# Preparing the first unit of a fused convolution and gated MLP: convolution by bands and then turning, against turning and then diagonal taps on TensorE

## Chip, cores and metric

One core of a Trainium2 chip. The metric is the device time of one execution in microseconds; three runs of the kernel before took 705.06 to 705.57, median 705.33.

## The reference

x is (8, 4096, 192), weight (8 heads, 7 taps), w_in (192, 2048), w_out (2048, 192), all float32. In short:

```python
w = softmax(weight, axis=-1)                       # 8 heads x 7 taps
# causal convolution in time; channel d belongs to head d // 24
c[b, s, d] = sum_k w[d // 24, k] * x_padded[b, s + k, d]   # 6 zeros ahead of each sequence
h = c.reshape(32768, 192) @ w_in                   # 32768 x 2048
out = (h * cos(h)) @ w_out                         # 32768 x 192
```

## The kernel before

The 32768 tokens are cut into 32 units of 1024 (U) and each unit into two tiles of 512 tokens (T), so there are 64 tiles. x arrives token-major (128 tokens on the partitions). For the product with w_in the convolved unit must stand channel-major, in the tile cT (64 channels on each half of the partitions, three groups k of 64 channels). Units 0 to 3 are prepared in one way and later units in another; the change concerns unit 0 and the constants that are made before it.

A tile then runs as follows. mm1 (L503) makes eight products h0 to h7 of w_in with cT, six matmuls each on alternate halves of the rows, into an h buffer; there are three such PSUM buffers ("the ring"), which parts of convolutions use in turn too. ACT takes the sine of h + pi/2 (L510, "s0" to "s7"), DVE multiplies it with h into g (L514). mm2 (L552) multiplies g with w_out (wo, bfloat16, in two halves, cast from wo_f by POOL at L120, steps W0 and W1) in 64 steps a tile ("m12" is twelve steps); two PSUM banks of 512 columns (o_bank 0 and 1) hold its sums. Steps 0 to 15 of a tile need the first half of wo, step 16 the second.

The order on each engine is written out by hand. PE_FIRST and PE_ORDER list what PE is given, ACT_FIRST and ACT_ORDER what ACT and DVE are given, tile by tile; engines run their queues in order. Tokens used below: hN is mm1 number N (h0a, h0b its halves), m the mm2 steps, w filler products, K the casts of a unit of x by POOL (L219), W the casts of wo, d and c the band convolution of a later unit, D, X and Y the doubling, the turning by a DMA transpose and the mending of its edges, L the loads of a unit, r (before) the rest of unit 0's convolution, e with a name the copies out of PSUM that belong to it. The first line of PE_FIRST before is:

```
"K1 h0a h0b W0 h1 h2 h3 r h4 w5 d11 w4 h5 d21 W1 c11 X0 m1 h6 m11 h7 L2 c21 D1"
```

Before the first tile the kernel before does this. The softmax of the taps is made with two heads on each quarter of the partitions (L140 to L185: quarter, wmax, wexp, wsum, wn). prod and diag (L401, L404) form the taps along a diagonal, and sixteen small copies (L415), shared by DVE, POOL and ACT, put them into band, a banded matrix for each head. conv_first (L432) convolves the first four blocks of 128 tokens by 32 products with bands; two copies (L438) bring them to ct, turned by twelve products with an identity (L453) and copied to cT (L457). The other four blocks go through r (conv_rest, L465 and L472) and a DMA transpose X0 (L326). keep_warm (L136) issues products of zeros. w_in is loaded by POOL in two transfers (L112), one for each half of its columns, which are the two halves of the partitions of w. On SP the second half of unit 0 and the whole of unit 1 are released by diag, and w_out (L124) by conv_first's second copy.

Of the kernel before, what the change touches and what calls it, by code (L numbers as in the profile page):

```python
# [16 lines left out]
def kernel(  # L17
# [40 lines left out]

    xf = x.rearrange("b s d -> (b s) d")
# [20 lines left out]
    w_row = consts.tile([4, HQ * K], FP32)  # L80
    nc.scalar.dma_start(out=w_row, in_=weight.rearrange("(q h) k -> q (h k)", q=4))
# [26 lines left out]
    w_src = moe_w_in.rearrange("(m k) (t f) -> t m k f", k=NC, t=2)  # L108
    HP = NP // 2

    def load_w(t):
        nc.gpsimd.dma_start(out=w[64 * t : 64 * t + 64].rearrange("p k j f -> p k (j f)"), in_=w_src[t])  # L112

    load_unit(0, 0, NB)
# [12 lines left out]

    one = consts.tile([128, 1], FP32)
    nc.vector.memset(one, 1.0)
    zero = consts.tile([128, T], BF16)  # L130
    nc.vector.memset(zero, 0.0)  # L131
    idle = o_pools[0].tile([128, T], FP32, name="o_ps0")

    def keep_warm(n, bank=idle):
        for _ in range(n):
# [3 lines left out]
    quarter = consts.tile([4, 128], FP32)  # L139
    nc.gpsimd.memset(quarter, 1.0)  # L140
    nc.gpsimd.affine_select(out=quarter, in_=quarter, compare_op=ALU.is_ge, fill=0.0, base=0, pattern=[[1, 128]],
                            channel_multiplier=-32)
    nc.gpsimd.affine_select(out=quarter, in_=quarter, compare_op=ALU.is_ge, fill=0.0, base=31, pattern=[[-1, 128]],
                            channel_multiplier=32)
# [4 lines left out]
    w_bc = w_all[:, 0 : HQ * K].rearrange("p (h k) -> p h k", k=K)  # L149
    nc.tensor.matmul(out=w_all[:, 0 : HQ * K], lhsT=quarter, rhs=w_row, start=True, stop=True)  # L150
    keep_warm(9)


    xb0 = consts.tile([128, UB + 1, D], BF16, name="x_bf0")

    E = 32 + K - 1
    mask = consts.tile([128, E, K], BF16)
    nc.gpsimd.memset(mask[0:32], 0.0)
    nc.gpsimd.affine_select(out=mask[0:32], in_=mask[0:32], compare_op=ALU.not_equal, fill=1.0, base=1 - K,  # L159
                            pattern=[[1, E], [1, K]], channel_multiplier=-1)  # L160
    band = consts.tile([128, H, 256], BF16)
    nc.vector.memset(band, 0.0)
    for q, copy in enumerate((nc.vector.tensor_copy, nc.scalar.copy, nc.scalar.copy)):
        copy(out=mask[32 * q + 32 : 32 * q + 64], in_=mask[0:32])  # L164
    for t in range(2):
        load_w(t)
    nc.gpsimd.memset(xb0[:, 0, :], 0.0)
    ident = consts.tile([128, 128], BF16)
    nc.gpsimd.memset(ident, 0.0)
    nc.gpsimd.affine_select(out=ident, in_=ident, compare_op=ALU.not_equal, fill=1.0, base=0, pattern=[[1, 128]],  # L170
                            channel_multiplier=-1)
    wn = consts.tile([128, HQ, K], BF16)
    ct_bufs = [consts.tile([128, 2 * NC * NPB + 1, 64], BF16, name="ct_buf%d" % i) for i in range(2)]

    wmax = consts.tile([128, HQ, 1], FP32)
    nc.vector.tensor_reduce(out=wmax[:, :, 0], in_=w_bc, axis=mybir.AxisListType.X, op=ALU.max)
    wexp = consts.tile([128, HQ, K], FP32)
    nc.vector.tensor_tensor(out=wexp, in0=w_bc, in1=wmax.to_broadcast([128, HQ, K]), op=ALU.subtract)
    nc.scalar.activation(out=wexp, in_=wexp, func=AF.Exp)
    nc.scalar.activation(out=scrap, in_=one, func=AF.Sin)  # L180
    wsum = consts.tile([128, HQ, 1], FP32)
    nc.vector.tensor_reduce(out=wsum[:, :, 0], in_=wexp, axis=mybir.AxisListType.X, op=ALU.add)
    winv = consts.tile([128, HQ, 1], FP32)
    nc.vector.reciprocal(winv, wsum)
    nc.vector.tensor_tensor(out=wn, in0=wexp, in1=winv.to_broadcast([128, HQ, K]), op=ALU.mult)  # L185
    wo = consts.tile([128, NP, 2, D], BF16)

# [19 lines left out]
    def cast_unit(u, n0=0, n1=UB + 1, copy=nc.gpsimd.tensor_copy):  # L207
        if u >= FIRST_RAW:
            xk[u] = xk_pool.tile([128, NC * (UB + 1), 64], BF16, name="xk")
            for n0, n1 in ((NPB, UB + 1), (0, NPB)):  # L210
                copy(out=xk[u][:, NC * n0 : NC * n1].rearrange("p (k n) m -> p k n m", k=NC),  # L211
                     in_=x_tiles[u][:, n0:n1].rearrange("p n (m k) -> p k n m", k=NC))
            if u % UPS == 0:
                nc.gpsimd.memset(xk[u][0 : 128 - OP, 0 : NC * NPB : NPB], 0.0)
            return
        if n0 == 0:
            bf[u] = xb0 if u == 0 else xbf_pool.tile([128, UB + 1, D], BF16, name="x_bf")
        o = 1 if u == 0 else 0
        copy(out=bf[u][:, n0 + o : n1 + o, :].rearrange("p n (h k r) -> p (n h) k r", k=NC, r=R),  # L219
             in_=x_tiles[u][:, n0:n1, :].rearrange("p n (h r k) -> p (n h) k r", k=NC, r=R))  # L220

    ct_tiles = {}
    have = {("whole", 0, 0)}
# [24 lines left out]
    def conv_part(u, c, banks, whole=False):  # L248
# [6 lines left out]
        if u == 1 and c == 0:  # L255
            spread_taps(ps[1][:, nb * 2 * G : nb * 2 * G + K])
# [4 lines left out]
        for b in range(2):  # L261
            conv_out(u, c, ps, 0, 0, nb, nc.scalar.copy, banks=(b,))
            if b and u == 1 and c == 0:
                nc.scalar.copy(tap, ps[1][:, nb * 2 * G : nb * 2 * G + K])
# [44 lines left out]
    def turn_unit(u, n0=0, n1=UB + 1, part=0):  # L309
# [12 lines left out]
        have.update((("turn", u), ("whole", u, 1)) if u == 0 else (("turn", u),))  # L322
# [9 lines left out]
    pick = consts.tile([128, 2, 2, 4, 2, R], BF16)  # L332

    def spread_taps(ps):

        for i in range(2):
            nc.tensor.matmul(out=ps, lhsT=pick[:, i].rearrange("p t q i r -> p (t q i r)"), rhs=wn[:, i, :],
                             start=i == 0, stop=i == 1, skip_group_check=True)

# [12 lines left out]
    def taps(u, j, half, mul):  # L352
        if u not in pa:
            pa[u] = pa_pool.tile([128, PA, WN, OR], FP32, name="pa")
        part = slice(HALF * half, HALF * (half + 1))
# [4 lines left out]
    def conv_raw(u):  # L360

        a, p = pa.pop(u), raw_prod
# [26 lines left out]
    def mend_edges(u):  # L389
# [6 lines left out]


    cast_unit(0, 0, NB, nc.scalar.copy)

    prod = consts.tile([128, HQ, E, K], BF16)  # L400
    nc.vector.tensor_tensor(out=prod, in0=mask.rearrange("p (o e) k -> p o e k", o=1).to_broadcast([128, HQ, E, K]),  # L401
                            in1=wn.rearrange("p h (o k) -> p h o k", o=1).to_broadcast([128, HQ, E, K]), op=ALU.mult)
    diag = consts.tile([128, HQ, E], FP32)
    summed = nc.vector.tensor_reduce(out=diag, in_=prod, axis=mybir.AxisListType.X, op=ALU.add)  # L404

    tc.add_manual_dep(nc.sync.nop().ins, summed.ins.name, sync_dep, reason="order of the transfers")
    load_unit(0, NB, UB)
# [3 lines left out]

    three = {"D": nc.vector.tensor_copy, "A": nc.scalar.copy, "P": nc.gpsimd.tensor_copy}
    for i, k in enumerate("DPDPDPDPDPDPDPAA"):
        q, rows = divmod(i, 4)
        three[k](out=band[32 * rows : 32 * rows + 32, HQ * q : HQ * (q + 1), 32 * rows : 32 * rows + E],  # L415
                     in_=diag[32 * q : 32 * q + 32])
    cast_unit(0, NB, UB)
    nc.gpsimd.memset(pick, 0.0)
    for i in range(2):
        nc.gpsimd.affine_select(out=pick[:, i, :, :, i, :], in_=pick[:, i, :, :, i, :], compare_op=ALU.not_equal, fill=1.0,  # L420
                                base=0, pattern=[[0, 2], [-32, 4], [0, R]], channel_multiplier=1)
    ct_tiles[0] = ct_pool.tile([128, UB + 1, NC, 2, 64], BF16, name="ct")
    cT[0] = cT_pool.tile([128, NC * (UB + 1) * 128], BF16, name="cT")
    copies = [nc.scalar.copy, nc.vector.tensor_copy]

    def conv_first():

        banks = o_banks()
        for half in range(2):
            for h in range(H):  # L430
                for prev in range(2):
                    nc.tensor.matmul(  # L432
                        out=banks[half][:, 0 : 2 * D].rearrange("p (n k h r) -> p h n k r", n=2, k=NC, h=H)[:, h],
                        lhsT=band[:, h, 128 * prev : 128 * prev + 128],
                        rhs=bf[0][:, 2 * half + 1 - prev : 2 * half + 3 - prev, h * G : (h + 1) * G].rearrange(
                            "p n (k r) -> p n k r", k=NC),
                        start=(h == 0 and prev == 0), stop=(h == H - 1 and prev == 1), skip_group_check=True)
            m = copies[half](out=ct_tiles[0][:, 2 * half : 2 * half + 2].rearrange("p n k t w -> p (n k) t w"),  # L438
                             in_=banks[half][:, 0 : 2 * D].rearrange("p (m t w) -> p m t w", t=1, w=64).to_broadcast(
                                 [128, 2 * NC, 2, 64]))  # L440
        tc.add_manual_dep(nc.sync.nop().ins, m.ins.name, sync_dep, reason="order of the transfers")
        load_wo(0)
        load_wo(1)

    def turn_first(half):
# [280 lines left out]
```

## Time and profile before

| | us |
|---|---|
| median of three runs | 705.33 |
| the profiled execution | 705.18 |
| its span | 703.5 |
| PE busy in the span | 697.0 |
| DVE, ACT, POOL busy | 642.4, 644.4, 503.7 |
| first product with w_in (L503) starts | 10.60 |
| first sine (L510) starts | 11.14 |
| second half of wo cast (L120) | 21.12 to 22.59 |
| first product of tile 1 starts | 22.98 |

Times inside the span count from its start. The profile is that of one execution; the time around the span is 1.68 us. A row of the timeline gives start, duration, engine, line, operation, what is written and read, and in brackets how long the engine had been idle and what ended that. A run of equal instructions is one row, and its duration runs to the last one's end.

### The profile page before, as it was taken

What the parts mean: (1) busy time and instruction counts of PE and PEld (TensorE: products, weight loads), DVE (VectorE), ACT (ScalarE), POOL (GpSimd) and SP (SyncE); (2) the same over time, 40 slices, a digit from 0 to 9 for tenths busy, and PEclk for the clock granted to TensorE, in tenths of its full rate; (3) what the DMA queues carried; (4) which work ended last, traced back from release to release, by engine and by line L of the source; (5) the groups of instructions that cost most, each with busy time, mean ns of one, the idle gap of its engine ahead of it and who ended that gap; (6) DMA issues with size and microseconds to landing.
All of it is one profiled execution on the core that took longest, in us unless ns stands there. A gap on an engine that the chain in (4) does not pass through costs nothing.

```text
span 703.5 us, 26826 instructions
## 1 busy us (share of the span) xinstructions
PE 697.0 (99%) x11830; PEld 512.8 (73%) x11830; DVE 642.4 (91%) x598; ACT 644.4 (92%) x831; POOL 503.7 (72%) x214
## 2 busy tenths in 40 slices
PE   8999999999999999999999999999999999999997
PEld 4677777777777777777777777777777777777776
DVE  6889999999999999999999999999999999999996
ACT  7889999999999999999999999999999999999875
POOL 6524478977778877778877688877789778799400
PEclk9999999999999999999999999999999999999999
DMA  8964456667667768676656577577665576874331
GB/s 214 234 167 97 120 135 143 138 147 164 138 153 146 131 145 176 134 152 131 147 152 153 150 159 129 140 161 150 143 147 132 145 174 137 153 127 95 92 91 47
DMA packets 228292, 100.09 MB, mean 142 GB/s; under 512 B 156240, under 2 KB 227792, under 8 KB 228176
## 3 DMA queue, kind: packets, MB, share of 16 engines
q1 hardware_dynamic: 227464, 97.40, 62.7%
q8 instruction: 92, 1.51, 0.9%
q0 software_dynamic: 416, 0.79, 0.7%
q14 instruction: 24, 0.20, 0.1%
q10 hardware_dynamic: 296, 0.20, 0.1%
HBM read 31.36 MB, written 25.17 MB: 80 GB/s over the span
## 4 chain that ended last, share of the span: by engine, by line
PE 96%; DMA 1%; DVE 1%; POOL 0%; SPq 0%; ACT 0%; issue 0%; POOLq 0%
PE o_ps L552 48%; PE h L503 46%; PE h L277 2%; DMA wo_f<-in_moe_w_out_dram 1%; PE h L552 0%; SPq L124 0%; PE h L229 0%; DVE band L415 0%; POOL wo L120 0%; POOL mask L159 0%; DVE ct L438 0%; PE o_ps L432 0%; ACT mask L164 0%; DVE diag L404 0%; DVE prod L401 0%
## 5 line engine op out<-in xcount | busy, mean ns | idle before, releaser
L514 DVE TENSOR_TENSOR g<-h,cs 128x1024 bf16<-128x1024 f32 (+1 forms) x513 | 604.9, 1216 | 27.9 <-ACT cs L510 24.5
L510 ACT ACTIVATE cs<-h 128x1024 bf16<-128x1024 f32 (+1 forms) x513 | 511.0, 1021 | 44.0 <-PE h L503 30.6
L552 PEld LDWEIGHTS <-g 64*128 64x128 bf16 x8192 | 354.2, 94 | 102.2 <-issue 1.0
L552 PE MATMUL o_ps<-wo,g 64*128 64x192 bf16 x8128 | 420.6, 243 | 0.1
L503 PE MATMUL h<-cT,w 64*128 64x512 bf16 (+1 forms) x3078 | 407.0, 376 | 0.8 <-DVE g L514 0.4
L503 PEld LDWEIGHTS <-w 64*128 64x128 bf16 x3078 | 147.6, 94 | 75.0 <-issue 1.8
L211 POOL CAST xk<-x_f 128x768 bf16<-128x768 f32 (+1 forms) x56 | 76.4, 1367 | 113.9 <-DMA x_f<-in_x_dram 109.3
L363 POOL TENSOR_TENSOR raw_prod<-rT,tap 128x2784 f32<-128x2784 bf16 x28 | 135.3, 4832 | 0.2
L370 POOL TENSOR_TENSOR raw_prod<-raw_prod,pa 128x2088 f32<-128x2088 f32 x28 | 129.1, 4609 | 2.2
L356 ACT ACTIVATE pa<-rT,tap 128x348 f32<-128x348 bf16 x168 | 94.6, 580 | 0.0
L374 POOL TENSOR_TENSOR raw_prod<-raw_prod 128x1392 f32<-128x1392 f32 x28 | 87.9, 3138 | 2.2
L571 DVE COPY o_sb<-o_ps 128x384 f32<-128x384 f32 x62 | 34.6, 557 | 23.7 <-PE o_ps L552 23.5
L377 POOL TENSOR_TENSOR ro<-raw_prod 128x696 bf16<-128x696 f32 x28 | 46.5, 1660 | 2.2
L294 ACT CAST ct_buf<-h 112x480 bf16<-112x480 f32 x56 | 28.6, 562 | 4.1 <-PE h L277 0.6
L571 ACT COPY o_sb<-o_ps 128x384 f32<-128x384 f32 x64 | 30.8, 482 | 0.1
L277 PE MATMUL h<-xk,band 64*112 64x120 bf16 x448 | 21.2, 213 | 0.0
L277 PEld LDWEIGHTS <-band 64*112 64x112 bf16 x448 | 18.0, 127 | 0.0
L219 POOL CAST x_bf<-x_f 128x768 bf16<-128x768 f32 (+2 forms) x5 | 9.1, 1812 | 7.0 <-DMA x_f<-in_x_dram 6.9
L307 POOL COPY ct<-ct 128x1728 bf16<-128x1728 bf16 x3 | 4.9, 1630 | 8.9 <-ACT ct L239 8.9
L394 POOL COPY cT<-cT 128x144 bf16<-128x144 bf16 x3 | 0.9, 308 | 13.5 <-DMA cT<-ct 13.5
L136 PE MATMUL o_ps<-zero 128*128 128x512 bf16 x21 | 7.2, 492 | 1.3 <-DVE zero L131 1.3
L239 ACT CAST ct<-h 128x432 bf16<-128x432 f32 x12 | 5.9, 530 | 0.4 <-issue 0.4
(66 smaller groups left out, 52.7 us busy)
## 6 DMA issues: line engine op xcount, KB each, us to landing
out_dram<-o_sb SPq DMA_DIRECT2D x63, 384.0 KB, 3.7
x_f<-in_x_dram SPq DMA_DIRECT2D x28, 480.0 KB, 5.5
x_f<-in_x_dram SPq DMA_DIRECT2D x56, 192.0 KB, 2.7
cT<-ro SPq DMA_DIRECT2D x112, 87.0 KB, 2.3
x_f<-in_x_dram SPq DMA_DIRECT2D x4, 384.0 KB, 5.6
wo_f<-in_moe_w_out_dram SPq DMA_DIRECT2D x4, 384.0 KB, 7.9
x_f<-in_x_dram SPq DMA_DIRECT2D x2, 768.0 KB, 5.2
cT<-ct_buf SPq DMA_TRANSPOSE x56, 4.0
```

The source lines that it names most:

```text
L211: copy(out=xk[u][:, NC * n0 : NC * n1].rearrange("p (k n) m -> p k n m", k=NC), in_=x_tiles[u][:, n0:n1].rearrange("p n (m k) -> p k n m", ...
L277: return nc.tensor.matmul(out=ps[h // 4][0:OP, 0 : NPB * 4 * G].rearrange("p (m i r) -> p i m r", m=NC * NPB, i=4)[:, h % 4], lhsT=band[si ...
L356: mul(pa[u][:, j, part], tap_window(u, j)[:, part], tap[:, j : j + 1])
L363: nc.gpsimd.tensor_tensor(out=p, in0=tap_window(u, PA, K), in1=tap[:, PA:K].rearrange("p (j a b) -> p j a b", a=1, b=1).to_broadcast([128, ...
L370: add(out=p[:, 0:m], in0=p[:, 0:m], in1=a[:, done : done + m], op=ALU.add)
L374: add(out=p[:, 0:m], in0=p[:, 0:m], in1=p[:, n - m : n], op=ALU.add)
L377: add(out=ro[u], in0=p[:, 0], in1=p[:, 1], op=ALU.add)
L503: nc.tensor.matmul(out=h[:, i, n0 * 128 : n1 * 128], lhsT=w[rows, k, j, :], rhs=rhs, start=(k == 0), stop=(k == NC - 1))
L510: nc.scalar.activation(out=cs[:, :, part], in_=h[:, :, part], func=AF.Sin, bias=math.pi / 2.0, scale=1.0)
L514: nc.vector.tensor_tensor(out=g_tiles[t][:, 2 * j : 2 * j + 2, part], in0=h[:, :, part], in1=cs[:, :, part], op=ALU.mult)
L552: ms.append(nc.tensor.matmul(out=o_ps[tt, b, si], lhsT=g_tiles[tt][rows, f, s * 128 : (s + 1) * 128], rhs=wo[rows, f // 2, f % 2, :], star ...
L571: (copy or copies[b])(o_sb[t][:, 2 * b : 2 * b + 2, :].rearrange("p s d -> p (s d)"), o_ps.pop((t, b)))
```

## The change

Unit 0 is turned first and convolved afterwards. Four casts by ACT (cast_first) bring pairs of blocks to xb0, grouped by channel; turn_pair turns a pair by products with the identity, and sets the six tokens ahead of each block in front of it; DVE or ACT copies the result to xT. diag now holds, for each tap, a diagonal matrix of that tap's weight for 64 channels, twice side by side. conv_pair convolves a pair by fourteen products (seven taps, two halves of the rows, two banks) of 384 columns, and the copies go straight to cT. Pairs 0 and 1 are done ahead of tile 0, pairs 2 and 3 inside it, as v2 and v3. r, X0 and ct of unit 0 go. The softmax has one (head, channel) row on each partition, with the sum taken by the Exp itself. The bands, now needed for units 1 to 3 only, are made after the first pairs, with all sixteen copies on POOL. The taps of later units (tap) are copied from wn by POOL instead of being spread by products. The load of unit 0 is three transfers in a row at the start; w_in comes in four transfers, two ahead of the identity and two after pick; unit 1 and w_out are released by the second copy of pair 0. Filler products fall from 21 to 7. The marks p and q in the order lists go, and the step they marked is found by counting.

The diff, cut:

```diff
-    w_row = consts.tile([4, HQ * K], FP32)
+    w_row = consts.tile([H, K], FP32)
...
-    load_unit(0, 0, NB)
+    def load_w(t, a):
+        nc.gpsimd.dma_start(out=w[64 * t : 64 * t + 64, :, a * HP : (a + 1) * HP].rearrange("p k j f -> p k (j f)"), in_=w_src[t, a])
+
+    load_unit(0, 0, NB // 2)
+    load_unit(0, NB // 2, NB)
+    load_unit(0, NB, UB)
...
+    nc.gpsimd.affine_select(out=head, ...)
+    for t in range(2):
+        load_w(t, 0)
+    nc.gpsimd.affine_select(out=ident, ...)
+    for q in range(4):
+        nc.gpsimd.tensor_copy(out=wide[32 * q : 32 * q + 32, K - 1 : K + 31], in_=ident[32 * q : 32 * q + 32, 32 * q : 32 * q + 32])
+    nc.gpsimd.tensor_copy(out=pick..., in_=...)
+    for t in range(2):
+        load_w(t, 1)
...
+    nc.tensor.matmul(out=w_bc, lhsT=head, rhs=w_row, start=True, stop=True)
+    keep_warm(WARM[0])                      # 3
+    nc.vector.tensor_reduce(out=wmax, in_=w_bc, axis=mybir.AxisListType.X, op=ALU.min)
+    nc.scalar.activation(out=wexp, in_=w_bc, func=AF.Exp, bias=wmax, scale=-1.0, accum_out=wsum)
...
+    def cast_first(n0, n1, copy):
+        copy(out=xb0[:, :, n0 + 1 : n1 + 1, :].rearrange("p k n m -> p n k m"),
+             in_=x_tiles[0][:, n0:n1, :].rearrange("p n (m k) -> p n k m", k=NC))
+    def turn_pair(p, ps):
+        for k in range(NC):
+            for prev, t0, t1 in ((0, EDGE, EDGE + 128), (1, 0, EDGE)):
+                n = 2 * p + 1 - prev
+                nc.tensor.matmul(out=to[:, k, t0:t1], lhsT=xb0[:, k, n : n + 2, :]..., rhs=ident[:, 128 - (t1 - t0) : 128], ...)
+    def conv_pair(p, ps):
+        for j in range(K):
+            for i in range(2):
+                rows = slice(64 * i, 64 * i + 64)
+                nc.tensor.matmul(out=ps[i][:, 0 : NC * 128]..., lhsT=diag[rows, j]..., rhs=xT[rows, p, :, j : j + 128],
+                                 start=j == 0, stop=j == K - 1)
+    def conv_later(p, cs):
+        ps = conv_pair(p, [o_bank(0), o_bank(1)])
+        yield
+        for i in range(2):
+            conv_copy(p, i, ps, copies[cs[i]])      # ACT, then DVE
+            yield
+    cast_first(0, 2, nc.scalar.copy)
+    to = turn_pair(0, o_bank(1))
+    keep_warm(WARM[1])                      # 1
+    make_diag(0, 4)
+    nc.vector.tensor_copy(out=xT[:, 0], in_=to)
+    cast_first(2, 4, nc.scalar.copy)
+    nc.scalar.activation(out=scrap, in_=one, func=AF.Sin)
+    make_diag(4, K)
+    to = turn_pair(1, o_bank(0))
+    nc.vector.tensor_copy(out=xT[:, 1], in_=to)
+    ...                                     # two products with pick into wb
+    ps0 = conv_pair(0, [ring_banks()[0], ring_banks()[0]])
+    nc.scalar.copy(out=wh, in_=wb...)
+    cast_first(4, 6, nc.scalar.copy)
+    cast_first(6, 8, nc.scalar.copy)
+    nc.vector.tensor_tensor(out=prod, ...)
+    rest = [turn_pair(2 + i, rest[i]) for i in range(2)]
+    conv_copy(0, 0, ps0, copies[0])
+    m = conv_copy(0, 1, ps0, copies[1])
+    ps1 = conv_pair(1, [o_bank(0), o_bank(1)])
+    for i in range(2):
+        nc.scalar.copy(out=xT[:, 2 + i], in_=rest[i])
+    nc.gpsimd.tensor_copy(out=tap, in_=wn)
+    nc.vector.tensor_reduce(out=bands, in_=prod, ...)
+    conv_copy(1, 0, ps1, copies[0])
+    conv_copy(1, 1, ps1, copies[1])
+    tc.add_manual_dep(nc.sync.nop().ins, m.ins.name, sync_dep, reason="order of the transfers")
+    load_unit(1, 0, NB)
+    load_unit(1, NB, UB)
+    load_edges(1)
+    load_wo(0)
+    load_wo(1)
+    for i in range(16):
+        q, rows = divmod(i, 4)
+        nc.gpsimd.tensor_copy(out=band[32 * rows : 32 * rows + 32, HQ * q : HQ * (q + 1), 32 * rows : 32 * rows + E],
+                              in_=bands[32 * q : 32 * q + 32])
...
-    PE_FIRST = ["K1 h0a h0b W0 h1 h2 h3 r h4 w5 d11 w4 h5 d21 W1 c11 X0 m1 h6 m11 h7 L2 c21 D1",
+    PE_FIRST = ["K1 h0a h0b h1 v2 h2 h3 v3 W0 h4 d11 h5 d21 W1 c11 m1 h6 m11 h7 L2 c21 D1",
...
-    ACT_FIRST = ["s0a s0b s1 s2 er s3 s4 ed11 ed21 s5 ec11 s6 ec21 s7",
+    ACT_FIRST = ["s0a s0b s1 ev2 ev2 s2 s3 ev3 ev3 s4 ed11 ed21 s5 ec11 s6 ec21 s7",
```

More of the change, by code (lines that the diff above doesn't have):

```diff
@@ L161 @@
[L161 to L171, printed above, removed]
@@ L422 @@
[L422 to L443, printed above, removed]
```

209 lines of the change are left out of this document (91 added, 118 removed), and 13 rows, old and new, of tables (ACT_FIRST, PE_FIRST).

## The prediction

> **What bounds it now.** The page first: TensorE (PE) is busy 697.0 of 703.5 us, so the steady state is PE's, and the change touches none of it: behind the first tile every queue holds the same instructions in the same order. A gain or a loss can only come from how soon PE reaches its unbroken run. The chain of waits, cut to the first 45 us, shows where that run begins:
>
> ```profile
> 9.89 0.38 SPq L124
> ...
> 12.16 8.84 DMA wo_f<-in_moe_w_out_dram
> ...
> 21.12 1.48 POOL wo L120
> 22.60 0.04 issue
> 22.64 0.34 PE o_ps L552 x4
> 22.98 0.65 PE h L503 x6
> ```
>
> Columns: start, duration, what. From 22.64 on the chain is PE to the end; before it stand the loads of w_out, released late, and their cast. I therefore compare kernels at one mark: the first product of tile 1, 22.98 here. Next, the timeline by engine, for what would have held PE without w_out:
>
> ```profile
> 3.24 3.48 PE L136 MATMUL o_ps<-zero 128*128 128x512 bf16 x9
> ...
> 8.71 0.59 PE L136 MATMUL h<-zero 128*128 128x512 bf16 x2
> ...
> 10.60 1.62 PE L503 MATMUL h<-cT,w 64*128 64x256 bf16 x18 [0.18 <-DVE cT L457]
> ...
> 21.41 0.82 PE L503 MATMUL h<-cT,w 64*128 64x512 bf16 x6 [0.15 <-DVE g L514]
> ```
> ```profile
> 5.55 1.21 ACT L219 CAST x_bf<-x_f 128x768 bf16<-128x768 f32 x1
> ...
> 11.14 3.26 ACT L510 ACTIVATE cs<-h 128x512 bf16<-128x512 f32 x4 [0.37 <-PE h L503]
> 14.47 1.50 ACT L472 CAST ct<-o_ps 128x768 bf16<-128x768 f32 x2
> ...
> 22.27 1.02 ACT L510 ACTIVATE cs<-h 128x1024 bf16<-128x1024 f32 x1 [0.42 <-PE h L503]
> ```
> ```profile
> 11.73 1.23 POOL L219 CAST x_bf<-x_f 128x768 bf16<-128x768 f32 x1 [3.59 <-DMA x_f<-in_x_dram]
> ...
> 17.35 1.47 POOL L120 CAST wo<-wo_f 128x1536 bf16<-128x1536 f32 x1 [0.78 <-DMA wo_f<-in_moe_w_out_dram]
> 21.12 1.47 POOL L120 CAST wo<-wo_f 128x1536 bf16<-128x1536 f32 x1 [2.31 <-DMA wo_f<-in_moe_w_out_dram]
> ```
>
> The first sine (s0a) starts at 11.14, h7 of tile 0 at 21.41, held by DVE's g of three ring buffers earlier. So tile 0 is a relay PE, ACT, DVE through three PSUM buffers, and w_out cost little more: PE wanted it some 0.3 before it came.
>
> **Part 1, up to the first sine.** I walk every queue in its order; each step starts at the end of the one ahead or 0.04 after what it waits for. Before: taps, prod, diag (5.28 to 5.98), band copies to 7.9, 32 products, two copies of 0.8 and 0.96, turns, two copies, s0a at 11.14. That chain goes. In its place:
> - Warm products start at 1.4 (before 1.31; DVE has one memset more ahead), the tap product ends near 3.35, the minimum 3.4 to 3.55, Exp at 3.6 for 0.22. That Exp now also sums: no row shows this; between 0 and +0.2 (the DVE sum that goes, 0.17), taken as 0.
> - ACT: L219 takes 1.21 for 768 elements and an activation of one element 0.20, so 384 elements take 0.71 and let the next start after 0.61. Two casts end near 5.0. The Sin table and its scrap take 1.40 (4.14 to 5.54 now). Small copy wh 0.2, then casts 3 and 4, from 6.5 to 7.85.
> - PE: a turn of a pair is three 128-column and three 6-column products, 0.22 (six of L453 take 0.34). A pair's convolution is 14 products of 384 columns on alternate row halves and banks. The nearest row is L503: six of 512 on alternate halves in 0.65, so 0.216 a couple, here 0.162, times 7 = 1.14. If the halves did not overlap it were 2.28; I take 1.14, as the form is L503's. Pair 0 is done by 6.9, behind casts; turns 2 and 3 follow the casts, the last at 7.9; pair 1 ends at 9.25 (+0.17 drain).
> - Copies: ACT 0.48, DVE 0.56 (both L457), done at 10.0. First products 9.25 and 10.04, s0a at 9.83: **1.3 us earlier**.
>
> Covered here: the memset of band on DVE (0.91, ends 2.4, next wanted 3.4); make_diag (0.48 and 0.37 by L401's 532 in 0.48) under casts and table load; four wide copies, pick and tap on POOL, ending near 4.6 and 6.1, wanted 5.5 and after 14; the fillers, 14 fewer.
>
> **Part 2, the loads.** On SP the first x transfer now is three; its first two pieces are the 384 KB that landed 3.4 us after their issue at 0.82 (the tile view's shortest), so 4.2, in time for cast 2 at 4.3. The third competes with the first half of w_in, issued on POOL at 1.4 to 2.8 instead of 2.98 to 4.4 (two issues, 1.43). Alone it lands at 5.4 (384 KB at 328 GB/s, mean of 10 to 18 us in the table by windows); behind one w_in transfer near 6.5; behind both near 8. I take 6.5, since both are issued together. From 6.4 on each 0.1 us late costs 0.1. w_in's first half lands near 8 and is wanted at 9.25: whole w_in took 6.6 us after its second issue, half of it 3.3 to 5 behind 2.1 to 2.8. Its rows are now half as long, which no row prices: at no cost it has 1.2 to spare; at twice the time it lands at 10.5 and the mark gains 0.4 only. I take no cost, since x's rows, shorter still (768 bytes against 2048), pass at 328 GB/s. The second half is issued at 4.5 to 5.9 and lands near 10; h4 wants it at 15.
>
> x of unit 1 and w_out are issued after DVE's second copy (7.4; before, diag at 5.98 released x, ct at 9.86 w_out). Queue: w_in to 9.6, x 864 KB to 12.3, w_out 1536 KB to 17.0. The transpose of unit 0 (SP 16.00 to 19.92), in whose time w_out's last piece hung until 21.0, is gone, and with it the 3.9 us that the loads of unit 2 stood behind it. POOL: 16 band copies at 0.29 (seven took 2.00) from 8.05 to 12.6, casts of unit 1 to 15.3, W0 to 16.8, W1 at 17.5 to 19.0. PE wants W1 at 21.0. So **w_out no longer waits**, with 2 us to spare.
>
> **Part 3, tile 0.** Removed: conv_rest (PE 0.7, ACT 1.50), nine fillers (1.9, PE), the tap copy (ACT 0.23). Added: v2 and v3, 1.14 each on PE, and one copy each on ACT and DVE per pair, 0.4 and 0.5. A new wait: v3 needs both banks, and DVE's copy of v2 stands behind g1, so v3 starts at 14.0 with PE idle 0.57; h4 at 15.15, s4 at 16.0. d11 starts at 16.15 with unit 1 cast. c11 needs the buffer of g4 (18.3, PE idle 1.15), then h6, eleven steps, **h7 at 20.3**. Against s0a, tile 0 takes 0.2 longer, so 1.1 of 1.3 survive. From h7 to the mark: before 1.57, with the wait for w_out in it; now 0.65 plus six steps of 0.082, 1.14. Mark at **21.47, 1.5 earlier**.
>
> **Sum.** The profiled execution took 705.18, span 703.5 and 1.68 around it; the median is 0.15 above. 705.18 - 1.5 = 703.7, plus 0.15: **703.8**. After the mark the relay of DVE behind PE is the same (g7 moves 1.1, and the next DVE-held product, d12 at 31.9, hangs on h2 of tile 1, not on g7). Unit 1's turned tile was ready at 33.28 and wanted at 35.61; its inputs move earlier too.
>
> In what order the DMA engines serve x and w_in decides part 2. The trace speaks for order of arrival: x released at 5.98, behind w_in, kept POOL until 11.73, 5.7 us against 3.4 for the same bytes alone. The Trainium skill, page DMA: Bandwidth & Descriptors (section Queues, rings and completion order), states instead that an engine goes round its queues in turn, packet by packet. By that rule, which the 11.73 does not bear out, the time would be the first rival's.
>
> **Rivals.**
> 1. *x shares with w_in.* Sharing halves x's rate while both run: pieces 2 and 3 land near 5.3 and 7.2, casts 2 to 4 slip, the mark gains 0.7: 704.6. Third piece behind the whole first half, 8.1: no gain, 705.3. For: x's third piece and w_in are now issued within 1 us of each other, where 2.2 us lay between before. Against: the 11.73 above. Chance 0.25.
> 2. *PE's clock.* Nine products of L136 take 3.48, 0.39 each, and two later ones 0.59 with the last one's drain: half the pace until about 6.0, though the granted clock reads 1.00 in every row of the table by windows. The release came 4.7 us after the first product at 1.31; counted from the tap product at 3.3 instead, it would come at 8.0: the mark gains 1.0 (704.3). At 9.4, nothing (705.3). For: 14 fillers fewer. Against: from 1.4 to 6.0 the products still leave gaps of 0.4 in all. The Trainium skill, page TensorE: Matmul & The Clock Gate (Part 1), puts the release at the end of a free-running window of 3.4 us that was busy; by that it could fall anywhere up to 8 here, an estimate from the page; the one release in this trace fits it and cannot test it. Chance 0.12.
> 3. *POOL's bands, the slower side.* All 16 copies now sit on POOL ahead of unit 1's casts, and d11 sits ahead of h5 and every w_out product in PE's queue. At 0.29 each it fits; past 0.38 each d11 moves h5, and every 0.1 a copy more then costs 1.6. At 0.5, 705.7; at 0.6, 707.3. For: DVE and ACT shared them before, and DVE is busier now. Against: POOL's 768-element casts took the same 1.23 beside a busy DVE. Chance 0.08.
>
> **Numbers.** The forecast has 0.5, its own range 703.2 to 704.2: third piece early (-0.2), Exp's sum or a cast slower (+0.4). The remaining 0.05 is more gain: c11's wait of 1.15 partly gone, 702.8. The range 702.8 to 705.9 takes in rivals 1 and 2 and rival 3 at 0.5 a copy. Faster by over 0.2% (1.4 us, about what a measurement of this kernel can tell from no change) is below 703.9: the forecast but for its upper part (0.45) and the 0.05 of more gain, 0.5. Slower by as much, above 706.7: half of rival 3 (0.04) and, from rival 2, a clock released after 13 us, when the slow h products put the mark at 24.5 (0.03): 0.07. The rest, 0.43, is within.
>
> **What would show it.** Right: s0a near 9.8, no wait for w_out at W1, h7 near 20.3, mark near 21.5, the same run after it. Wrong: cast 3 waiting for x past 6.5; a convolution over 1.14; d11 waiting for POOL; w_out again ahead of PE in the chain; a wait after the mark that gives the gain back.

## The result and the profile after

The changed kernel took 708.34 to 709.98 us in four runs, median 708.78; the kernel before stands at 705.19 in the same comparison. The ratio is 1.0053 [1.0036, 1.0070]: slower by half a per cent, where 703.8 was forecast and 705.9 was the upper end. The profiled execution took 708.34 with a span of 706.5.

The mark, the first product of tile 1, moved from 22.98 to 25.84. Span less mark is 680.5 before and 680.7 after, so the whole loss lies ahead of the mark. (In the rows after, helpers stand a few lines lower: mm1 is L506, mm2 L555, the sine L513, cast_first L399, turn_pair L413, conv_pair L421.)

The chain of waits after, cut to the first 27 us; columns are start, duration, what:

```profile
1.78 7.88 DMA x_f<-in_x_dram
...
9.68 1.31 ACT x_bf L399 x2
...
11.04 0.56 PE h L413 x6
11.60 2.40 PE o_ps L421 x14
...
26.02 0.65 PE h L506 x6
```

Before, w_out stood ahead of PE. Now it is the third piece of unit 0's x, issued at 1.78 and in use at 9.68. Casts 3 and 4 wait for it, then the turns, convolution 1 and all of tile 0. The timeline by engine gives the sizes, ACT, PE and POOL in turn; brackets hold the idle time ahead and what ended it:

```profile
9.68 1.30 ACT L399 CAST x_bf<-x_f 128x384 bf16<-128x384 f32 x2 [2.98 <-DMA x_f<-in_x_dram]
...
14.58 2.26 ACT L513 ACTIVATE cs<-h 128x512 bf16<-128x512 f32 x3
```
```profile
10.43 0.40 PE L413 MATMUL h<-ident,x_bf 128*128 128x128 bf16 x6 [2.31 <-ACT x_bf L399]
...
11.53 2.42 PE L421 MATMUL o_ps<-xT,diag 64*128 64x384 bf16 x14
13.74 2.04 PE L506 MATMUL h<-cT,w 64*128 64x256 bf16 x18
15.62 1.31 PE L421 MATMUL o_ps<-xT,diag 64*128 64x384 bf16 x14
...
24.70 0.82 PE L506 MATMUL h<-cT,w 64*128 64x512 bf16 x6
...
25.84 0.83 PE L506 MATMUL h<-cT,w 64*128 64x512 bf16 x6
```
```profile
9.43 4.49 POOL L483 CAST band<-bands 32x76 bf16<-32x76 f32 x16 [3.18 <-DVE bands L472]
13.98 2.73 POOL L221 CAST x_bf<-x_f 128x768 bf16<-128x768 f32 x2
17.54 1.47 POOL L123 CAST wo<-wo_f 128x1536 bf16<-128x1536 f32 x1 [0.83 <-DMA wo_f<-in_moe_w_out_dram]
19.98 1.47 POOL L123 CAST wo<-wo_f 128x1536 bf16<-128x1536 f32 x1 [0.98 <-DMA wo_f<-in_moe_w_out_dram]
```

Two things went wrong on the way to the first sine, which starts at 14.58 instead of 9.83. Cast 3 starts 3.18 later than forecast. And convolution 1 takes 2.42 at 11.53, where 14 products of the same form, those of a later pair, take 1.31 at 15.62. The table by windows has the cause beside it (each row: the stretch and its length, busy time of PE, its weight loads, DVE, ACT and POOL, then granted clock, DMA share and GB/s):

```profile
8.00:10.00 2.00, 0.13 (x2) 0.00 (x0) 1.17 (x2) 0.32 (x1) 0.48 (x3) 1.00 1.05 177
10.00:12.00 2.00, 1.37 (x16) 0.96 (x18) 0.00 (x0) 1.73 (x4) 1.69 (x8) 0.74 1.03 289
12.00:14.00 2.00, 2.00 (x18) 0.92 (x14) 0.00 (x0) 0.54 (x3) 1.68 (x8) 0.50 0.97 246
```

PE was busy 0.13 of the 2 us from 8 to 10, and the clock granted then fell to 0.74 and 0.50. So the first theory, A: w_in's first half, now issued at 1.44 to 2.87 beside x's third piece (issued at 1.78), holds that piece back; PE stands idle for it, the clock falls, and these two make the loss. In the trace's records of the transfers, ten of the third piece's sixteen parts had landed by 6.81 and the other six between 8.51 and 9.66, while w_in's first half landed between 5.78 and 9.49. (A load lands in sixteen parts in these records, and has landed when the last one has.) Its rivals: the cost is in w_in's halved rows (1 KB written a piece instead of 2 KB); the clock falls by itself, for want of filler products; the relay of tile 0 is longer than forecast.

### The profile page after: what moved, and what is told of

Read it like the earlier page. It is cut to its first block, busy times and chain, and to the rows that moved or that the text cites. A ratio compares the mean times of both kernels' runs of the same rounds, so it can differ in the third digit from the quotient of the medians.

```text
span 706.5 us, 26833 instructions
## 1 busy us (share of the span) xinstructions
PE 698.1 (99%) x11833; PEld 531.8 (75%) x11833; DVE 642.9 (91%) x598; ACT 643.9 (91%) x832; POOL 504.3 (71%) x221
## 4 chain that ended last, share of the span: by engine, by line
PE 97%; DMA 1%; DVE 1%; ACT 0%; SPq 0%; issue 0%
PE o_ps L555 48%; PE h L506 47%; PE h L275 2%; DMA x_f<-in_x_dram 1%; PE o_ps L421 1%; PE h L555 0%; PE h L231 0%; DVE g L517 0%; ACT x_bf L399 0%; DVE cT L428 0%; ACT cs L513 0%; ACT ct L241 0%; SPq L103 0%; PE h L413 0%; DVE o_sb L584 0%
## 5 line engine op out<-in xcount | busy, mean ns | idle before, releaser
L513 ACT ACTIVATE cs<-h 128x1024 bf16<-128x1024 f32 (+1 forms) x513 | 510.8, 1021 | 43.7 <-PE h L506 29.8
L555 PEld LDWEIGHTS <-g 64*128 64x128 bf16 x8192 | 365.3, 94 | 91.5 <-issue 0.7
L555 PE MATMUL o_ps<-wo,g 64*128 64x192 bf16 x8128 | 426.3, 243 | 0.0
L506 PE MATMUL h<-cT,w 64*128 64x512 bf16 (+1 forms) x3078 | 412.6, 376 | 0.1
L506 PEld LDWEIGHTS <-w 64*128 64x128 bf16 x3078 | 160.6, 94 | 66.8 <-issue 0.7
L221 POOL CAST x_bf<-x_f 128x1728 bf16<-128x1728 f32 (+2 forms) x4 | 7.8, 1949 | 0.1
L483 POOL CAST band<-bands 32x76 bf16<-32x76 f32 x16 | 3.8, 240 | 3.8 <-DVE bands L472 3.2
```

Source lines behind the costliest of these rows:

```text
L506: nc.tensor.matmul(out=h[:, i, n0 * 128 : n1 * 128], lhsT=w[rows, k, j, :], rhs=rhs, start=(k == 0), stop=(k == NC - 1))
L513: nc.scalar.activation(out=cs[:, :, part], in_=h[:, :, part], func=AF.Sin, bias=math.pi / 2.0, scale=1.0)
L555: ms.append(nc.tensor.matmul(out=o_ps[tt, b, si], lhsT=g_tiles[tt][rows, f, s * 128 : (s + 1) * 128], rhs=wo[rows, f // 2, f % 2, :], star ...
```

## Experiments

Times are medians; each ratio is against the kernel before on the same chip.

**1. All of w_in behind x.** One edit to the changed kernel: the two transfers of w_in's first half move on POOL from ahead of ident to behind pick.

```diff
-    for t in range(2):
-        load_w(t, 0)                # ahead of ident
...
-    for t in range(2):
-        load_w(t, 1)
+    for c in range(2):
+        for t in range(2):
+            load_w(t, c)            # behind pick, 3.15 to 5.82
```

> The changed kernel with all four w_in transfers issued behind pick, at about 3.3 us instead of 1.4. Theory A (w_in's first half takes the bandwidth of x's third piece; the cold clock only follows from the wait): cast 3 starts near 6.6 instead of 9.68, no stretch of granted clock under 1.00, first sine near 10, first product of tile 1 at 21.5 to 22.5, time 704 to 705. Rival B (w_in's rows of half the length load the DMA engines whenever they pass): cast 3 still past 8, time above 707.

Measured: 705.62, ratio 1.0006 [0.9997, 1.0016], mark 22.55. ACT, PE and POOL:

```profile
6.59 1.32 ACT L398 CAST x_bf<-x_f 128x384 bf16<-128x384 f32 x2
```
```profile
8.30 1.32 PE L420 MATMUL o_ps<-xT,diag 64*128 64x384 bf16 x14
...
16.90 0.53 PE L230 MATMUL h<-x_bf,band 128*128 128x216 bf16 x4 [0.65 <-POOL x_bf L220]
...
19.78 0.26 PE L554 MATMUL o_ps<-wo,g 64*128 64x192 bf16 x2 [0.79 <-POOL wo L123]
```
```profile
15.37 1.48 POOL L220 CAST x_bf<-x_f 128x960 bf16<-128x960 f32 x1 [0.99 <-DMA x_f<-in_x_dram]
...
18.26 1.47 POOL L123 CAST wo<-wo_f 128x1536 bf16<-128x1536 f32 x1 [1.41 <-DMA wo_f<-in_moe_w_out_dram]
20.74 1.47 POOL L123 CAST wo<-wo_f 128x1536 bf16<-128x1536 f32 x1 [1.01 <-DMA wo_f<-in_moe_w_out_dram]
```

Cast 3 starts at 6.59 without a wait, convolution 1 takes 1.32 and the granted clock is 1.00 throughout: 3.2 of the 3.6 us come back by the place of two DMA issues alone. A holds for the first sine, though the time lies 0.6 above the 705 that I expected at most: 1.1 us to the forecast's mark of 21.47 are still missing. The rows show PE's waits for late loads: d11 0.65, the first product of w_out 0.79. The last of unit 1's loads to land is its smallest, the edges (L88, 96 KB), at 15.24; POOL's second cast starts at 15.37.

**2. The clock alone.** Ten filler products behind convolution 0 in the changed kernel, so that PE has work while it waits.

```diff
+    keep_warm(10, o_bank(0))
```

> The changed kernel with ten filler products behind pair 0's convolution, so that PE is busy while x's third piece is awaited. Theory A with the clock as second part: cast 3 stays at 9.7, granted clock 1.00 throughout, pair 1's convolution 1.3 instead of 2.4 us, time 1.4 to 1.8 less than the changed kernel, near 707.2. Rival C (the wait alone explains it, the clock costs nothing): 708.8.

Measured: 708.03, ratio 1.0044 [1.0029, 1.0059], mark 25.16. In this execution x came 0.55 later still:

```profile
10.23 1.32 ACT L399 CAST x_bf<-x_f 128x384 bf16<-128x384 f32 x2 [3.54 <-DMA x_f<-in_x_dram]
```
```profile
11.94 1.32 PE L421 MATMUL o_ps<-xT,diag 64*128 64x384 bf16 x14
```
```profile
10.00:12.00 2.00, 1.96 (x21) 1.10 (x20) 0.00 (x0) 1.70 (x3) 1.69 (x8) 1.00 0.95 227
```

With the clock at 1.00, convolution 1 is back at 1.32. From the start of cast 3 to the first h it takes 2.87 here (10.23 to 13.10) and in run 1 (6.59 to 9.46), but 4.06 in the changed kernel: the clock costs 1.19, and x's delay the other 3.09 (9.68 less 6.59). In the median the fillers bring 0.75 only, as x is no sooner; the executions of the two kernels overlap in time, so the 1.19 rests on these rows. So the clock is a part of the loss, smaller than I expected, and a consequence of the late x.

**3. Whole rows, early.** The changed kernel with w_in in whole rows, both transfers at the early place.

```diff
-    w_src = moe_w_in.rearrange("(m k) (t a f) -> t a m k f", k=NC, t=2, a=2)
+    w_src = moe_w_in.rearrange("(m k) (t f) -> t m k f", k=NC, t=2)
```

> The changed kernel with w_in in whole rows, two transfers, both at the place of the first half. Theory A: x's third piece still shares with w_in, cast 3 at 9 to 10, w_in whole by 10, time 708 to 709. Rival B (short rows are what slows x and w_in): cast 3 before 8, time 706 to 707.

Measured: 711.42, ratio 1.0087 [1.0072, 1.0102], mark 28.98.

```profile
12.59 1.30 ACT L397 CAST x_bf<-x_f 128x384 bf16<-128x384 f32 x2 [5.89 <-DMA x_f<-in_x_dram]
```

The halved rows fall as the cause: with rows of full length x is held back to 12.59, later than the 9 to 10 expected, and the time is 2.4 above the upper end. (All of w_in now stands beside x instead of half of it, so the run doesn't price the row length by itself.)

**4. The same fault put into the kernel before.** There x's second half and unit 1's x are released by wmax near 3.5 instead of the sum at 5.98.

```diff
-    tc.add_manual_dep(nc.sync.nop().ins, summed.ins.name, ...)
+    tc.add_manual_dep(nc.sync.nop().ins, early.ins.name, ...)     # early = the reduce that makes wmax
```

> The kernel before with the second half of unit 0 (and unit 1) released by wmax at 3.5 us instead of diag at 5.98, so that its packets arrive when w_in has just begun. If the DMA engines serve in order of arrival: POOL's cast of it still near 11 or later, first product with w_in still 10.6, time 705.2. If they go round the queues: cast near 9, w_in landing 1 us later, first product near 11.5, time 705.5 to 706.5.

Measured: 708.41, ratio 1.0041 [1.0026, 1.0056], mark 25.99.

```profile
12.70 1.47 PE L503 MATMUL h<-cT,w 64*128 64x256 bf16 x17 [1.82 <-DMA w<-in_moe_w_in_dram]
14.61 2.74 PE L503 MATMUL h<-cT,w 64*128 64x512 bf16 x12 [0.43 <-DVE g L514]
```

x's second half is cast at 10.52 instead of 11.73, so it is served among w_in's pieces and not behind them; w_in lands at 12.65 instead of 10.4, the first h waits 1.82 for it, and the kernel before loses 3.2 us too. That is more than either expectation had: the clock stands beside the wait, 0.50 from 14.09 to 17.50, and the twelve products at 14.61 take 2.74, where they took 1.47 before. In these kernels transfers issued at about the same time share, both ways.

**5 to 7. Where the rest went: rows and release.** All with w_in behind pick, as in run 1. Run 5 uses whole rows (two transfers). Run 6 keeps the halves and releases unit 1's x and w_out by the second make_diag (6.2) instead of the convolution's copy (7.75). Run 7 does both.

```diff
...
-    make_diag(4, K)
+    early = make_diag(4, K)
...
-    tc.add_manual_dep(nc.sync.nop().ins, m.ins.name, sync_dep, reason="order of the transfers")
+    tc.add_manual_dep(nc.sync.nop().ins, early.ins.name, sync_dep, reason="order of the transfers")
```

> w_in in whole rows again, two transfers of 128 rows' halves as in the kernel before, both issued behind pick on POOL (the place that had four transfers of half rows in the kernel with all of w_in behind pick, whose mark stood at 22.55). Theory A (x's third piece was late only because w_in was in flight beside it; what is left to the forecast's 21.47 is lost because x of unit 1 and w_out end late, behind a w_in that moves slowly in 1 KB pieces): cast 3 at 6.6 as there; two issues end near 4.6; in 2 KB pieces (173 ns each in the trace of before, 16 engines, 768 KB) w_in takes 4.1 us and has landed near 10.0, as late as the first half alone there (9.9), so the first h does not move; x of unit 1 lands near 12.7 instead of 14.6, w_out near 17.5 instead of 19.9; POOL waits for neither, W1 at 17.6 to 19.1; d11 without its wait of 0.65, first product of w_out without its wait of 0.79; mark 21.5 to 22.0, time 704.1 to 704.7. Rival D (length of rows costs nothing, the generation of descriptors or the issue sets w_in's pace): whole w_in lands near 12.0, the first h waits for it until then, s0a 12.5, mark 24.6, time 707.6.

> w_in in four transfers of half rows behind pick, and x of unit 1 and w_out released by the second make_diag on DVE (ends near 6.2) instead of the second convolution copy (ends near 7.8 in that kernel). Theory A with queues served in turn: the two queues share from about 8.2 instead of 9.9; w_in's first half lands 0.6 to 1.0 later (10.5 to 10.9 against 9.9), s0a near 11.1, x of unit 1 lands near 12.8, w_out near 18.3; what the late loads give back is lost at the first h: mark 22.3 to 22.8, time 705.3 to 705.8. Rival E (w_in alone leaves the engines idle for a good third of 5 to 9 us, and the released loads only fill these gaps): w_in's first half lands at 9.9 as before, x of unit 1 by 12.3, w_out by 17.8, s0a 10.4, no wait at d11, mark 21.6 to 21.9, time 704.2 to 704.8.

> Whole rows of w_in behind pick, and x of unit 1 and w_out released by the second make_diag. Theory A with queues served in turn: w_in shares from 8.2 on and lands near 10.8 to 11.3 instead of 10.0; the first h waits, s0a 11.3 to 11.8, mark 22.5 to 23.0, time 705.4 to 706.0, later than with whole rows alone. Rival E (only gaps are filled): w_in near 10.0, x of unit 1 12.2, w_out 17.0, mark 21.4 to 21.7, time 704.0 to 704.5. If w_in comes no sooner in whole rows than in halves (Rival D): s0a past 12.5, mark past 24.6, 707.6 or more.

Measured: 709.86 (1.0054 [1.0035, 1.0073], mark 27.60), 705.77 (1.0008 [0.9999, 1.0018], mark 22.43) and 709.07 (1.0053 [1.0036, 1.0070], mark 27.08). Run 5, PE:

```profile
14.33 2.74 PE L504 MATMUL h<-cT,w 64*128 64x256 bf16 x17 [2.69 <-DMA w<-in_moe_w_in_dram]
```

Run 6, windows:

```profile
6.00:8.00 2.00, 1.70 (x23) 1.04 (x21) 1.84 (x5) 1.99 (x6) 0.24 (x1) 1.00 0.88 118
8.00:10.00 2.00, 2.00 (x26) 1.13 (x26) 0.81 (x2) 1.52 (x4) 1.21 (x6) 1.00 0.93 122
```

My expectation for whole rows was wrong by some 4 us: w_in landed at 14.29 in the profiled execution, the longest of run 5 (710.13, the shortest 707.07), not at 10.0, and Rival D's 12.0 was nearer. In run 7 it landed at 13.04, and the difference of the two is within the scatter. With unit 1's x under way, w_in got 38 KB in half a microsecond and less from 10.0 on in run 5, against 73 to 109 KB for x. The halves therefore earn their place: the first h needs only the first one, and that landed at 9.83 in run 1.

Run 6's time and mark lie inside Theory A's range by luck: SP issued unit 1's x at 6.23, but its first bytes moved at 10.16, as in run 1 (issued 7.77, first bytes 10.22), so w_in was not slowed, as A has it, and nothing filled the time, as E has it. In the kernel before and in runs 1, 5, 6 and 7 an x issued when w_in's issues were over moved its first bytes when 536 to 698 of w_in's 768 KB had moved, and shared with the rest. With the DMA engines nearly idle (runs 11 and 12) it took 1.03 from the issue to the first bytes. Issued beside w_in's own issues, x shared from early on (runs 3 and 4). What in the queues makes this difference was not tried.

**8 to 10. Other orders.** Run 8: w_in's second half behind the tap copy on POOL, with the early release. Run 9: also four of the sixteen band copies on DVE. Run 10: also the release by the first make_diag (near 5.0).

```diff
     nc.gpsimd.tensor_copy(out=tap, in_=wn)
+    for t in range(2):
+        load_w(t, 1)                                # run 8
...
+    for i in range(4):
+        make_band(i, nc.vector.tensor_copy)         # run 9; POOL keeps 12
...
-    make_diag(0, 4)
+    early = make_diag(0, 4)                         # run 10
```

> The first half of w_in behind pick, the second half behind the small copy of the taps on POOL (6.2 to 7.5 instead of 4.5 to 5.8), x of unit 1 and w_out released by the second make_diag as in the run before. Theory A, as the last three runs left it (w_in occupies all 16 engines for 5.2 to 5.8 us, and a transfer that is queued once w_in's descriptors are in gets next to nothing until w_in is through): now x of unit 1 stands beside or ahead of w_in's second half; w_in's first half lands by 9.0 to 9.7, x of unit 1 near 11.5 to 12.5 instead of 14.4, the second half near 12.5 to 13.5 (wanted near 15 by h4), w_out near 18 to 18.5; POOL's casts of unit 1 follow the bands without a wait (13.1 to 16.0), d11 without its wait of 0.85, W0 at 16.5 to 17.5, W1 near 18.5 to 19; mark 21.5 to 21.9, time 704.2 to 704.7. Rival F (the engines' total work until w_out sets the mark, whatever the order): w_out still ends near 19.5 to 20, W1 at 20.3 or later, mark 22.3 or later, time 705.3 or more.

> As the kernel with the second half of w_in behind the taps' copy, and four of the 16 band copies moved from POOL to DVE, into its idle time of 1.2 us ahead of its copy of convolution 1 (0.25 us each). Theory A: POOL's bands end near 12.0 instead of 13.1; if x of unit 1 has landed by 12.5, its casts end near 14.9, W0 is cast by 17.5 and W1 by 20; mark 0.1 to 0.3 earlier than without the move, time 704.0 to 704.5. Rival F: POOL only waits longer for the loads, the mark does not move.

> As the kernel with four bands on DVE, with x of unit 1 and w_out released by the first make_diag (ends near 5.0) instead of the second (near 6.2). Theory A with arrival at the engines deciding: issued at 5.0 to 6.6, behind w_in's first half (issues end at 4.4) and ahead of its second, x of unit 1 lands by 11, the first half of w_in at 9.0 to 9.9 as before, mark 0 to 0.2 earlier, time 703.9 to 704.5. Rival G (queues that hold work at the same time share): x of unit 1 shares with w_in's first half, which lands at 10.5 to 11.5; the first h waits, s0a 11 to 12, mark 22.4 to 23.2, time 705.3 to 706.1.

Measured: 705.38 (1.0004 [0.9996, 1.0013], mark 23.20), 705.53 (1.0012 [1.0003, 1.0020], mark 22.75), 705.60 (1.0008 [1.0000, 1.0017], mark 23.71). In none did the mark come below run 6's 22.43, and no time fell into Theory A's ranges; Rival F's "705.3 or more" fits all three. The marks are of one execution each, and the medians lie within 0.4 of those of runs 1 and 6, less than a kernel's executions differ among themselves. So these runs don't rank the orders.

Run 10 shows sharing in the records of the transfers: x, issued at 5.07 among w_in's issues, moved its first bytes at 7.12, and while it moved 67, 87 and 78 KB per half microsecond from 8.5 to 10.0, w_in fell from 57 KB to 38, 31 and 27. Unit 1's first transfer of x was in use 0.77 sooner than in run 9 (13.36 against 14.13), w_in's first half landed at 10.82 instead of 9.37, and W1 started at 21.87 instead of 20.91. That is Rival G's way, by the bytes; the landing times alone don't show it, for in run 8, where x moved nothing before 10.30, the first half landed at 10.75 too. No order tried makes a kernel faster than the one before.

**11 to 14. The loads taken away.** To see whether the loads alone stand between run 1 and the forecast, only a half (run 11) or a quarter (run 12) of w_in's columns is loaded, behind pick, and read by every h; run 13 is the kernel before with that quarter, run 14 is run 12 with the early release.

```diff
-    w_src = moe_w_in.rearrange("(m k) (t a f) -> t a m k f", k=NC, t=2, a=2)
+    w_src = moe_w_in.rearrange("(m k) (t a f) -> t a m k f", k=NC, t=2, a=4)     # only a = 0 is loaded
...
-        ... lhsT=w[rows, k, j, :] ...
+        ... lhsT=w[rows, k, j % 2, :] ...
```

> As the kernel with all of w_in behind pick (mark 22.55, s0a 10.41), but the second half of w_in's columns is not loaded at all; the products of h4 to h7 read the first half's columns instead, in every tile, so 768 KB less are read and the instructions of PE are the same in number and shape. Rival F (what is left to the forecast is the DMA engines' total work up to w_out): first half and s0a as there (9.9, 10.4); x of unit 1 lands near 12.3, w_out near 17.6; POOL waits for neither, d11 and the first product of w_out lose their waits of 0.65 and 0.79; h7 10.5 after s0a, 20.9, mark 22.0, time 704.4 to 704.6. Rival H (tile 0's own relay is longer than the forecast made it, the late loads only fill its slack): mark 22.4 or later, time 705.2 to 705.7 as there.

> As before, with only the first quarter of w_in's columns loaded, behind pick, and read by every h: w_in then lands near 6.8 to 7.5, ahead of any want. Rival F: s0a at the forecast's 9.8, x of unit 1 by 11.5, w_out by 16.5, h7 20.3, mark 21.5, time 703.8 to 704.0: the forecast's own sum, once the loads are out of the way. Rival H: s0a 9.8 but h7 more than 11 after it, mark 22.0 or later, time 704.5 or more.

> The kernel before with the same quarter of w_in loaded (at its own place, 2.98 to 4.4) and read by every h. If the change shortens the chain by what the forecast says, this kernel, whose loads are as much out of the way, keeps its band chain: s0a 11.1 as before, w_out landed by 15 ahead of the transpose, no wait for W1, h7 21.4, mark 22.5, time 704.7 to 705.0, so that the change is worth 1.0 with the loads out of the way. If the kernel before was itself held by x and w_in (its cast of x's second half waited 3.59), s0a or h7 come earlier too: mark 21.7 to 22.0, time 704.0 to 704.3, and the change is worth 0.5 or less even so.

> A quarter of w_in's columns loaded and read by every h, as in the run with the release at the convolution copy (mark 22.18, first product of w_out waiting 0.33, w_out landed 20.3, s0a 10.38 with convolution 0 at half pace), and x of unit 1 and w_out released by the second make_diag near 6.2. Rival F (the end of the loads holds the mark): x of unit 1 lands by 11.5 and w_out by 17.7, no wait at POOL's casts of w_out nor at the first product, h7 10.5 after s0a; with s0a at 10.0 to 10.4 the mark is at 21.6 to 22.0, time 704.0 to 704.4. Rival H (tile 0's relay): w_out lands as early, the mark stays at 22.2 or later, 704.6.

Measured: run 11 704.51, 0.9992 [0.9982, 1.0001], mark 22.06. Run 12 704.62, 0.9994 [0.9984, 1.0003], mark 22.18, not the 21.5 expected. The DMA engines stood nearly idle where the release had not come yet. The windows of run 12 (columns as above):

```profile
6.00:8.00 2.00, 2.00 (x20) 1.06 (x16) 1.26 (x3) 1.89 (x5) 0.00 (x0) 1.00 0.30 37
8.00:10.00 2.00, 2.00 (x32) 1.39 (x32) 1.17 (x2) 1.37 (x3) 0.47 (x2) 1.00 0.07 11
```

Of the 0.66 to run 14's mark 0.31 lies behind the first sine (10.66 to h7 against 10.35), where the late release counts, and 0.35 ahead of it (10.38 against 10.03), where convolution 0's 13 products took 1.97 instead of 1.59 and pushed convolution 1 from 8.30 to 8.65.

Run 13: 704.99, 0.9997 [0.9988, 1.0007], mark 22.54; h7 stayed at 21.40 and W1 at 18.12 was long in time, so w_out's wait was worth 0.44 to the kernel before. Run 14: 704.45 (704.01 to 705.48), 0.9993 [0.9983, 1.0002]; its profiled execution took 704.06 and has the mark at 21.52. Its chain, cut, holds no DMA:

```profile
8.37 1.30 PE o_ps L419 x14
9.67 0.02 issue
9.69 0.57 DVE cT L426
...
14.35 2.35 DVE g L515 x2
...
21.20 0.49 PE o_ps L553 x12
21.70 0.65 PE h L504 x6
```

The rows of s0a, h7 and the mark in run 14, and of the mark in run 13:

```profile
10.03 0.60 ACT L511 ACTIVATE cs<-h 128x512 bf16<-128x512 f32 x1
```
```profile
20.38 0.82 PE L504 MATMUL h<-cT,w 64*128 64x512 bf16 x6
...
21.52 0.83 PE L504 MATMUL h<-cT,w 64*128 64x512 bf16 x6
```
```profile
22.54 0.83 PE L503 MATMUL h<-cT,w 64*128 64x512 bf16 x6
```

Here the forecast's mark is met to 0.05, with s0a at 10.03 and h7 at 20.38. In that execution the chain of compute comes to the forecast's sum, with s0a 0.20 late and the way from it to h7 0.12 shorter. In run 1 the loads keep the kernel from it: its missing 1.03 against run 14 splits by the rows into 0.38 up to the first sine (10.41 against 10.03: w_in's first half at 9.83) and 0.65 behind it (11.00 from s0a to h7 against 10.35: unit 1's x and w_out).

## Why the prediction was wrong

**Part 2, the third piece of x: the failing step.** "Behind one w_in transfer near 6.5": cast 3 started at 9.68. The choice rested on order of arrival, read from POOL's wait until 11.73, and on x standing behind one transfer of w_in at most. Runs 1, 3 and 4 show sharing where issues lie together. Rival 1 named the mechanism with 0.25, but ended it at 8.1, behind the whole first half; the piece came 1.6 later, and w_in's second half was landing from 8.09 on as well. From 6.5 to 9.5 x moved 3 to 21 KB in half a microsecond beside 50 to 85 KB of w_in, far less than a half. Why ten parts came early and six late is open. The row that misled was a true one: in the kernel before x was issued at 6.01, behind w_in's issues, and its first bytes moved at 9.34, when 698 of w_in's 768 KB were in; unit 1's x in run 6, issued 3.9 us before it moved, waited in the same way. What held for a transfer issued when w_in's issues are over was carried over to one issued beside them. The Trainium skill, page DMA: Bandwidth & Descriptors, section Queues, rings and completion order, says that an engine serves its queues in turn, a packet of several descriptors at a time; the 9.68 agrees with it, the 10.16 of run 6 does not look like turns.

**The price of a late piece.** "From 6.4 on each 0.1 us late costs 0.1" left out PE's clock: 3.09 of delay cost 4.28 at the first h (13.74 against 9.46 in run 1), the other 1.19 being the granted clock at 0.50 (run 2). Rival 2 looked for the clock at the start of the kernel, not behind a new idle time.

**Part 2, w_in and w_out: mis-sized.** Forecast were w_in's halves near 8 and 10, unit 1's x to 12.3, w_out to 17.0, W1 by 17.5 to 19.0 with "2 us to spare". With x out of the way (run 1) w_in's halves landed at 9.83 and 11.91, x's two large transfers at 13.04 and 14.50, its edges at 15.24, w_out at 20.62, and W1 ran from 20.74 to 22.21. w_in moves 118 to 122 GB/s while the engines are 0.88 to 0.93 busy (windows of run 6, 6 to 10 us), where 328 was read before from stretches of x and w_out; the forecast took x's rate as evidence that w_in's short rows cost nothing. The view of before had it already: from 6 to 8 us, where only w_in moved, it read

```profile
6.00:8.00 2.00, 1.36 (x15) 0.56 (x13) 1.73 (x7) 1.26 (x3) 1.57 (x7) 1.00 0.94 134
```

These are bytes written. w_in is float32 in memory and bfloat16 in w, so a piece of 1 KB has 2 KB read for it: as an estimate 49 ns per KB read (98 over 2), against 48 for x (36 for 0.75 KB). By that most of the gap to 328 is the bytes read, which the forecast left out when it queued w_in as 768 KB; the traces don't show the reading side. In place of 2 us to spare POOL waited 1.41 and 1.01 for w_out at W0 and W1, and PE 0.79 for W0.

**Part 1: right but for the turn.** Exp with its sum took 0.27 and 0.19 for reading the sum, the casts 0.70 each, a convolution 1.30 to 1.32 with its drain (1.14 + 0.17 was forecast). s0a came at 10.03 in run 14 against 9.83. Of these two tenths 0.09 are cast 3, at 6.59 instead of 6.5, and 0.12 the last turn, which took 0.34 up to convolution 1's start (7.96 to 8.30 in run 1) where 0.22 was forecast. Convolution 0's 13 products took 1.59 in run 14, 1.95 after, 1.97 in run 12 and 1.30 in run 1, as PE is slower at the start: the records of the granted clock begin, with 1.00, at 4.81 in run 1, 6.79 in run 14 and 7.5 in the other two, and the page reads 1.00 ahead of that too. That cost time only in run 12; in runs 1 and 14 convolution 1 starts at 8.30 alike. (The fillers fell from 24 to 7, by 17 and not by 14; no run puts them back at the start.)

**Part 3: right.** h7 came 10.12 after s0a, forecast 10.47; in run 14 10.35, 0.12 less than forecast. From h7 to the mark 1.14 was forecast and 1.14 measured, after and in runs 1, 11, 12, 13 and 14. POOL's sixteen band copies took 4.49, 0.28 each, so rival 3 was out. Behind the mark nothing was given back or lost: span less mark lies between 680.5 and 681.0 in all sixteen profiles.

**What the change is worth.** With the loads out of the way in both kernels the marks differ by 1.02 (22.54 less 21.52); with the 0.44 of w_out's wait, which the quarter removes from the kernel before too, that is 1.46, of 1.5 forecast. These are marks of one execution each, and run 14's is among its shortest; the medians of runs 13 and 14 differ by 0.54 only, and run 14's ratio is not clear of 1. That the mark was met to 0.05 is in part luck, by the late s0a and the short way behind it.

**The sum's last step.** "Profile plus 0.15" also fell short: run 14's median lies 0.39 above its profiled execution, run 1's 0.53. Executions of the changed kernels differ by 1.4 us and more (run 1: 704.86 to 706.24, run 10: 705.17 to 708.29), those of the kernel before by 0.5. The loads aren't shown as the cause: run 14's differ by 1.5, and what lengthens them no profile here shows.

## What to carry to other kernels

An edit that moves a load earlier is priced by what else holds the DMA engines at that moment: list every transfer with its issue time, and let those issued together share before letting any of them wait its turn. When a shorter chain of compute brings little, remove most of the load (a quarter of the weights, read again), release the others early and look whether the chain reaches its own sum; that tells a wrong chain from late data, if enough executions are profiled. And a wait on the path of TensorE costs more than its length when the granted clock falls behind it, as it did after and in runs 3 and 4.

## What the hardware showed

- After idle time of PE the granted clock fell, so that it was paid for twice: from 8.1 to 10.4 it did nearly nothing, and the granted clock read 0.74 from 10 to 12 and 0.50 from 12 to 14; with 5.09 us of idle time (run 3) it stayed at 0.50 to 18. The clock's records change in steps of 3.41 us. Where PE had been busy for 0.99 (after), 0.46 (run 3) and 1.60 (run 4) of the 3.41 us ahead of such a step, half the clock followed; where it had been busy for 1.81 (run 10) and 2.48 (run 1), full clock did.
- A casting load keeps the engines busy for little: w_in's 768 KB written took them from 4.80 to 11.91 in run 1. A piece of 1 KB took 98 ns in the median, one of 2 KB 173, one of x's 768 bytes 36.
- Unit 1's x, issued at 6.23 in run 6, moved its first bytes at 10.16, and in run 1, issued at 7.77, at 10.22; with the engines nearly idle (runs 11 and 12) it took 1.03 from issue to first bytes.
